# Three rewritten turns in a fused attention, experts and mixer kernel: first subtractions of two mixer pieces, one router product, three weight pieces

## The chip, the cores and the metric

One core of a Trainium2 chip runs the whole kernel as one program. The metric is the device time of one execution in microseconds (us); lower is better.

The engines are named TensorE (PE, its weight loads PEld), VectorE (DVE), ScalarE (ACT), GpSimd (POOL) and SyncE (SP, which here only issues transfers). Each runs its own instructions in order. "L1039" is line 1039 of the kernel.

## The reference

Three layers follow one another, on 2 sequences of 768 tokens with 512 channels.

```python
# attention: 8 heads of 64, 8 global keys and the last 96 keys, a slope per head
scores = q @ k.T / sqrt(64) - slope * dist          # kept keys only
x = softmax(scores) @ v
# experts: 8 experts, one for each token, by a scan over the sequence
fresh = argmax(x @ w_gate);  gate = sigmoid(x @ w_local)
e[s] = fresh[s] if s == 0 or gate[s] < 0.5 else e[s - 1]
x = p[e] * (relu(x @ w1[e]) @ w2[e])                # 512 -> 1024 -> 512
# mixer
u = x + real(fft(fft(x, axis=sequence), axis=channels))
un = (u - mean) / sqrt(var + 1e-6)
out = u + relu(un @ w_ch1) @ w_ch2                  # 512 -> 2048 -> 512
```

## The kernel before

**Split weights.** Each weight matrix is held as two parts, `hi` (a cast, on ScalarE) and `lo` (raw minus `hi`, one subtraction, L1039), and products are summed over hi*hi, hi*lo and lo*hi. `Ring.take` yields after every cast and every subtraction of one piece, so its caller decides in which place of the order each of them stands; its last step, once the raw buffer is free, issues the load of the piece four further on, from SP. Its `eng` says which engine subtracts.

**Attention** goes over 24 units (6 tiles of 128 tokens, 2 sequences, 2 groups of 4 heads), numbered n = 0 to 23. In the loop over n a unit passes through `scores` (TensorE, L133), `rowmin` (VectorE, L142), four exponentials (`expo`, ScalarE, L151), transposes `transp` in two halves (TensorE, L161), `out`, which copies each half out of PSUM to `p` (ScalarE, L167), `values` (TensorE, L175, into the upper half of the PSUM tile `sm`), `keep` (VectorE, L180), `upright` (L185) and `norm`. The units overlap: iteration n issues, in this order, `out(n-2)` second half, `keep(n-3)`, `scores(n)`, `rowmin(n)`, turn 0, first half of `transp(n-1)`, `expo(n)`, `out(n-1)` first half, turn 1, second half of `transp(n-1)`, `upright(n-3)`, `norm(n-3)`, turn 2, `values(n-2)`, turn 3. A turn is a call of `step(k)` with k = 4(n - 24) + turn. In it every background generator goes one yield further.

Two kinds of background work matter here. `Route.run(i)` is the router of tile i: it waits with `to(s)` for turn s and issues some small instructions there. For the fifth tile (i = 4, `soon`) its start is in iteration 22. The product of the gates with a unit matrix (L537, L538) goes into the lower half of `sm`; ScalarE copies it to `rows` (L541) and takes a small `exp` (L542); then come the scans `ex` (L552) and `cu` (L561) on VectorE and later the scatter of the tile's tokens to their experts' lists (L593, GpSimd). The other kind is `take` of expert 0's first three weight pieces, in quarters of 512 columns: cast on ScalarE (L1037), subtraction on GpSimd. `TAKES` gives the k at which each piece begins; a cast and a subtraction alternate from turn to turn. Their raw loads are issued in iterations 8, 12 and 16.

**The experts** follow (130 to 324 us), then the **mixer**. Its opening is an order written out by hand, `PLAN[1]`, a list of tokens; each token moves one generator by one step and names the engines of that step behind a colon (V VectorE, G GpSimd, A ScalarE):

- `f0` to `f5` fold a tile of the input (`sl0l` is the fold's `lo`, L1466)
- `q0`, `q1` are products over the sequence, `c` over the channels, `g` splits their results (`sl1l`, L1466)
- `w` is filler for TensorE
- `s` takes statistics, `k` is one instruction of the scales (the first is `v`, L1624), `n` normalises a tile to a row (L1648; `n1:A` on ScalarE, L1645), `t` turns it (transposes L1655 on TensorE, cast `un0h` and subtraction `un0l`, L1465 and L1466)
- `m0`, `m1` are the steps of the mixer's first two weight pieces: cast, subtraction, cast, subtraction (halves of 1024 columns), load. Piece 0 lies in `wide`, piece 1 in `sl5h` and `sl5l`
- `h` is the first half of the first hidden product (L1689).

The main loop then runs 48 steps, each with a hidden product (L1689, 12 matmuls of 512 columns), `hh` and `hl` (L1693 on ScalarE, L1694 on VectorE) and, after the next step's hidden product, the second product (L1703 with hh and hi, L1704 with hh and lo, L1705 with hl). Step 0 reads the first half of piece 0, step 1 the second half, steps 2 and 3 piece 1.

Of the kernel before, what the change touches and what calls it, by code (L numbers as in the profile page):

```python
# [60 lines left out]
def fast_attention(tc, st, io, route):  # L61
# [4 lines left out]
    with ExitStack() as ctx:  # L66
# [204 lines left out]
        def step(k):  # L271

            for at, g in TAKES:
                if k == at:
# [175 lines left out]
class Route:  # L450
# [31 lines left out]
    def run(self, i, xs, parts=None):  # L482
        nc, st, sb = self.tc.nc, self.st, self.sb
        V, A, G, T = nc.vector, nc.scalar, nc.gpsimd, nc.tensor
# [10 lines left out]
        last, first, soon = i == NT - 1, i == NT - 4, i == NT - 2  # L495
        X = V if last or soon else G
        to = lambda s, n=1: self.at(None if last else s, n)
# [31 lines left out]
        for b in range(B):  # L529
# [3 lines left out]
        X.tensor_tensor(pe, l8, m8[:, :, :1].to_broadcast([P, B, E]), op=ALU.subtract)  # L533
        V.scalar_tensor_tensor(gf, z.to_broadcast([P, B, E]), GATE, fr.to_broadcast([P, B, E]),
                               op0=ALU.is_lt, op1=ALU.mult)
        yield from to(1 if soon else 0, 2)
        T.matmul(rp[:, 0:P], gn.rearrange("p b e -> p (b e)"), self.identb, start=True, stop=True)  # L537
        T.matmul(rp[:, P:2 * P], gf.rearrange("p b e -> p (b e)"), self.identb, start=True, stop=True)  # L538
        rows = sb.tile([16, 2 * P], F32, name="rows")
        if not last:  # L540
            A.copy(rows, rp)  # L541
        A.activation(pe, pe, AF.Exp)  # L542
        yield from to(2 if soon else 1)
        V.tensor_reduce(out=su, in_=pe, op=ALU.add, axis=AX.X)
        if last:
            yield
# [2 lines left out]
        if last:  # L549
# [1 line left out]
        ex = sb.tile([16, P], F32, name="ex")  # L551
        V.tensor_tensor_scan(ex, rows[:, :P], (rp if last else rows)[:, P:], 0.0 if i == 0 else st.pe[:, P - 1:],  # L552
                             op0=ALU.mult, op1=ALU.add)
        yield from to(3 if soon else 2)
        V.reciprocal(su, su)
        oh = sb.tile([16, P], F16, name="oh")
        X.tensor_scalar(oh, ex, st.eid, None, op0=ALU.is_equal)
# [32 lines left out]
        for b in range(B):  # L590
            r = (i * B + b) * P
            nc.sync.dma_start(st.xs[r:r + P], xs[b])
            w = G.indirect_dma_start(  # L593
                out=st.list, out_offset=bass.IndirectOffsetOnAxis(ap=pos[:, b:b + 1], axis=0),
                in_=st.dest[:, b * NT + i], in_offset=None, bounds_check=E * LIST + P - 1, oob_is_err=False)
# [59 lines left out]
EARLY_READ = 7  # L655
EARLY_GATHER = 6
LATE = 4
TAKES = ((-43, 0), (-27, 1), (-19, 2))
SPLIT = 6
WARM = 6, 6, 3  # L660
LOAD = 6
# [4 lines left out]


PLAN = ("f0:VVVV f0:VV f0:V f1:VVVV f0:VV f1:VV", """
f2:VVVV f1:V f1:VV q0 m0:V q0 w w w q0 q0 f2:VV f2:V f2:VV q0 f3:VVVV f3:VV q0 g g g g g f4:VVVV m0:G w c c f4:VV c:VVVV c f3:V c
c:VVVV f3:VV c c s0 f5:VVVV f4:V f5:VV s1 s0 c c s3 s1 f4:VV s2 f5:V s3 s2 k k k q1 k q1 k m0 k k k k w q1  # L670
q1 k k f5:VV q1 k m1 n1:A n0:V n2:V n3:V m0:G t0 t1 g q1 m0 m1:G t2 t3 g g g m1 m1:G g m1 h
""")

DECODE, HALVE, ROOM, END = 4650, 1160, 4850, -1
# [1209 lines left out]
```

## Time and profile before

| | us |
|---|---|
| median of 3 runs | 644.39 (644.01 to 644.95) |
| profiled execution, its own time | 645.25 |
| its span, first to last instruction | 643.5 |
| attention and routing | 0 to 130 |
| experts | 130 to 324 |
| mixer's opening | 324 to 364 |
| mixer's main loop | 364 to 640 |

The profiled execution took 1.75 us more than its span. The mean granted TensorE clock over it was 0.997 of full speed. The stages are read from the timeline of TensorE.

### The profile page before, as it was taken

How to read it: one execution, taken by the hardware profiler on the slowest of the kernel's cores; microseconds unless marked ns; L12 is line 12 of the kernel's file. 1: busy time of each engine (PE TensorE's matmuls, PEld its weight loads, DVE VectorE, ACT ScalarE, POOL GpSimd, SP SyncE). 2: the span in 40 equal slices, each digit the busy share in tenths (PEclk: the TensorE clock that was granted, in tenths of full speed). 3: DMA queues.
4: the chain of work that ended last, by engine and by line, in shares of the span. 5: the costliest groups of instructions: out<-in, count | busy, mean ns of one | idle time of the engine just before them, and what ended most of it. 6: DMA issues, size and time to landing. Idle time of an engine off the chain costs nothing.

```text
span 643.5 us, 9998 instructions
## 1 busy us (share of the span) xinstructions
PE 618.0 (96%) x3634; PEld 506.6 (79%) x3635; DVE 390.0 (61%) x900; ACT 276.0 (43%) x550; POOL 111.0 (17%) x150
## 2 busy tenths in 40 slices
PE   8999988799999999999999799999999999999997
PEld 4777865498899898887867687888888888888885
DVE  5777786369875987671399877998531220272112
ACT  5788983166565565552434433541221221041110
POOL 2135562412333044210121300000000000000000
PEclk9999999999999999999999899999999999999999
DMA  8356584359887878863260143551100010100001
GB/s 304 154 200 135 135 191 158 76 181 325 317 324 258 300 248 348 347 213 115 96 261 7 66 138 125 197 196 67 65 1 1 1 67 0 66 0 1 0 1 65
DMA packets 25187, 92.45 MB, mean 144 GB/s; under 512 B 7644, under 2 KB 8796, under 8 KB 17184
## 3 DMA queue, kind: packets, MB, share of 16 engines
q1 hardware_dynamic: 19664, 79.50, 36.3%
q0 software_dynamic: 4736, 10.56, 4.5%
q10 hardware_dynamic: 720, 1.55, 0.7%
q8 instruction: 35, 0.57, 0.4%
q14 instruction: 32, 0.26, 0.2%
HBM read 81.00 MB, written 14.84 MB: 149 GB/s over the span
## 4 chain that ended last, share of the span: by engine, by line
PE 47%; issue 4%; DVE 2%; POOL 1%; ACT 0%; DVEq 0%; POOLq 0%; ACTq 0%
PE h L1689 21%; PE acc L1704 7%; PE acc L1703 7%; PE acc L1705 7%; PE y L1192 1%; PE f L1655 1%; PE more L1242 1%; PE more L1192 1%; PE h L1242 1%; PE f L1552 0%; PE f L1574 0%; POOL sl5l L1039 0%; POOL wide L1039 0%; DVE u L1714 0%; DVE fs L1477 0%
## 5 line engine op out<-in xcount | busy, mean ns | idle before, releaser
L1694 DVE SCALAR_TENSOR_TENSOR hl<-h,hh 128x512 fp32r<-128x512 f32 x48 | 33.1, 689 | 118.0 <-ACT hh L1693 117.8
L1693 ACT ACTIVATE hh<-h 128x512 fp32r<-128x512 f32 x48 | 28.7, 599 | 160.7 <-PE h L1689 160.6
L1039 DVE TENSOR_TENSOR wide<-raws,wide 128x1024 fp32r<-128x1024 f32 (+1 forms) x36 | 42.6, 1200 | 24.3 <-ACT wide L1037 23.8
L151 ACT ACTIVATE t<-t,nm 128x256 f32<-128x256 f32 (+1 forms) x96 | 45.8, 479 | 10.4 <-DVE nm L142 10.1
L1037 ACT CAST wide<-raws 128x1024 fp32r<-128x1024 f32 (+2 forms) x42 | 40.7, 990 | 6.3 <-PE acc L1705 3.4
L1689 PE MATMUL h<-un0h,wide 128*128 128x512 f32 (+1 forms) x136 | 42.5, 378 | 0.0
L1704 PE MATMUL acc<-wide,hh 128*128 128x512 f32 x96 | 37.8, 393 | 0.0
L1703 PE MATMUL acc<-wide,hh 128*128 128x512 f32 x96 | 37.6, 392 | 0.0
L1705 PE MATMUL acc<-wide,hl 128*128 128x512 f32 x96 | 37.5, 390 | 0.0
L142 DVE CUSTOM_DVE_ANT_0 t<-sp,bias 128x256 f32<-128x256 f32 (+1 forms) x96 | 33.0, 398 | 6.7 <-PE sp L133 3.5
L1122 POOL DMA_INDIRECT xg<-xs,ent x23 | 27.7, 1206 | 14.0 <-issue 6.4
L1212 PE MATMUL h<-xh,wide 128*128 128x256 f32 x192 | 28.5, 284 | 1.0 <-DVE hl L1216 0.8
L1215 ACT ACTIVATE hh<-h 128x512 fp32r<-128x512 f32 x28 | 16.7, 597 | 28.7 <-PE h L1212 21.6
L1689 PEld LDWEIGHTS h<-un0h,wide 128*128 128x128 f32 x136 | 25.0, 188 | 4.7
L161 PE MATMUL tp<-consts,t 128*128 128x128 f32 x176 | 26.4, 283 | 1.9 <-ACT p L167 1.5
L1212 PEld LDWEIGHTS h<-xh,wide 128*128 128x128 f32 x192 | 25.5, 191 | 2.0 <-DVE hl L1216 1.2
L161 PEld LDWEIGHTS tp<-consts,t 128*128 128x128 f32 x176 | 19.1, 140 | 9.9 <-ACT p L167 5.8
L175 PE MATMUL sm<-p,vs 128*64 128x128 f32 x352 | 24.5, 279 | 1.7 <-ACT rows L541 1.7
L1689 PE MATMUL h<-un0l,wide 128*128 128x512 f32 (+1 forms) x68 | 25.7, 378 | 0.0
L1216 DVE SCALAR_TENSOR_TENSOR hl<-h,hh 128x512 fp32r<-128x512 f32 x28 | 19.2, 686 | 9.2 <-issue 4.6
L167 ACT COPY p<-tp 128x512 f32<-128x512 f32 (+1 forms) x48 | 24.1, 536 | 1.2 <-PE tp L161 1.2
L175 PEld LDWEIGHTS sm<-p,vs 128*64 128x64 f32 x352 | 18.7, 136 | 5.5 <-issue 3.3
(461 smaller groups left out, 1662.4 us busy)
## 6 DMA issues: line engine op xcount, KB each, us to landing
raws<-we SPq DMA_DIRECT2D x31, 1024.0 KB
raws<-wm SPq DMA_DIRECT2D x18, 1024.0 KB
raws<-wmf SPq DMA_DIRECT2D x7, 1024.0 KB
wmf<-dec POOLq DMA_DIRECT2D x8, 512.0 KB
xs<-xrow SPq DMA_DIRECT2D x12, 260.0 KB
vs<-v SPq DMA_DIRECT2D x6, 512.0 KB
raws<-kq SPq DMA_DIRECT2D x3, 1024.0 KB
u<-x SPq DMA_DIRECT2D x6, 512.0 KB
```

The lines of the kernel that those rows point to most:

```text
L142: V.tensor_tensor_reduce(out=u.t[:, x, :u.W], in0=u.sp[:, j, k, :u.W], in1=bias[:, 4 * u.g + x, u.b0:u.b0 + u.W], scale=-0.125, scalar=3.0 ...
L151: A.activation(u.t[:, x, :u.W], u.t[:, x, :u.W], AF.Exp, bias=u.nm[:, x:x + 1], scale=-1.0, accum_out=u.den[:, x])
L161: T.transpose(u.tp[k][:, j, c], u.t[:, 2 * k + j, c * P:(c + 1) * P], st.ident)
L175: T.matmul(turned[j * D:j * D + D, k], vs[:, ti % KS, u.h + 2 * k + j], u.p[:, 2 * k + j, c], start=c == 0, stop=c == len(tiles) - 1)
L1037: (first or nc.scalar.copy)(hi[:, cs], raw[:, cs])
L1039: (eng() if callable(eng) else eng or nc.vector).tensor_tensor(lo[:, cs], raw[:, cs], hi[:, cs].bitcast(F32), op=ALU.subtract)
L1212: T.matmul(ps[:, u], w[:, f], x[:, k], start=n == 0, stop=n == 11)
L1689: nc.tensor.matmul(ps[:, c], a[:, k], x[:, k, c], start=n == 0, stop=n == 11)
L1694: nc.vector.scalar_tensor_tensor(hl, ps, 0.0, hh.bitcast(F32), op0=ALU.max, op1=ALU.subtract)
L1703: T.matmul(acc[c], hh[:, cs], h2, start=first, stop=False)
L1704: T.matmul(acc[c], hh[:, cs], l2, start=False, stop=False)
L1705: T.matmul(acc[c], hl[:, cs], h2, start=False, stop=last)
```

## The change

Three edits, all of them to the order of work.

1. In `PLAN[1]` three of the four subtractions of the mixer's pieces 0 and 1 are given to VectorE: piece 0's first, now ahead of fold 3; piece 0's second and piece 1's first, now behind the last turned rows (`t3`). Piece 1's second subtraction stays on GpSimd in its place. Piece 0's load follows its second subtraction as before.
2. In `Route.run`, for the fifth tile, the router products, the copy `rows` and the small `exp` are in turn 0 instead of 1, the sum and the scan `ex` in turn 1 instead of 2, the reciprocal and `oh` in turn 2 instead of 3.
3. In `TAKES` the three pieces of expert 0 begin at k = -53, -37 and -21 instead of -43, -27 and -19: iteration 10 turn 3, iteration 14 turn 3 and iteration 18 turn 3, instead of iteration 13 turn 1, 17 turn 1 and 19 turn 1.

```diff
-        yield from to(1 if soon else 0, 2)
+        yield from to(0, 2)
...
-        yield from to(2 if soon else 1)
+        yield from to(1)
...
-        yield from to(3 if soon else 2)
+        yield from to(2)
...
-TAKES = ((-43, 0), (-27, 1), (-19, 2))
+TAKES = ((-53, 0), (-37, 1), (-21, 2))
...
-f2:VVVV f1:V f1:VV q0 m0:V q0 w w w q0 q0 f2:VV f2:V f2:VV q0 f3:VVVV f3:VV q0 g g g g g f4:VVVV m0:G w c c f4:VV c:VVVV c f3:V c
+f2:VVVV f1:V f1:VV q0 m0:V q0 w w w q0 q0 f2:VV f2:V f2:VV q0 m0:V f3:VVVV f3:VV q0 g g g g g f4:VVVV w c c f4:VV c:VVVV c f3:V c
...
-q1 k k f5:VV q1 k m1 n1:A n0:V n2:V n3:V m0:G t0 t1 g q1 m0 m1:G t2 t3 g g g m1 m1:G g m1 h
+q1 k k f5:VV q1 k m1 n1:A n0:V n2:V n3:V t0 t1 g q1 t2 t3 m0:V g m1:V m0 g g m1 m1:G g m1 h
```

## Rows read from the trace of the kernel before

**Rows 1.** Page, part 1: busy us (share of the span) and instructions.

```profile
PE 618.0 (96%) x3634; PEld 506.6 (79%) x3635; DVE 390.0 (61%) x900; ACT 276.0 (43%) x550; POOL 111.0 (17%) x150
```

**Rows 2.** TensorE's timeline, 355 to 371: start, us, instruction, count, idle before.

```profile
355.75 0.33 PE L1515 MATMUL h<-wide,sl0l 128*1 128x386 f32 x1
359.94 1.09 PE L1655 MATMUL f<-consts,row 128*128 128x128 f32 x4 [3.85 <-issue]
...
370.54 0.39 PE L1705 MATMUL acc<-wide,hl 128*128 128x512 f32 x1
```

**Rows 3.** Windows 358 to 364: length, busy of each engine, PEclk, DMA, GB/s.

```profile
358.00:360.00 2.00, 0.06 (x1) 0.09 (x2) 1.84 (x9) 0.59 (x1) 0.00 (x0) 0.88 0.09 37
360.00:362.00 2.00, 2.00 (x10) 2.00 (x10) 1.07 (x3) 0.90 (x3) 0.00 (x0) 0.50 0.00 0
362.00:364.00 2.00, 2.00 (x13) 1.97 (x13) 1.53 (x3) 0.94 (x3) 0.00 (x0) 0.76 0.00 0
```

**Rows 4.** GpSimd's timeline, 330 to 368.

```profile
330.27 2.46 POOL L1039 TENSOR_TENSOR wide<-raws,wide 128x1024 fp32r<-128x1024 f32 x1 [2.45 <-ACT wide L1037]
351.81 2.43 POOL L1039 TENSOR_TENSOR wide<-raws,wide 128x1024 fp32r<-128x1024 f32 x1 [19.08 <-ACT wide L1037]
354.21 2.56 POOL L1039 TENSOR_TENSOR sl5l<-raws,sl5h 128x1024 fp32r<-128x1024 f32 x1
367.15 2.42 POOL L1039 TENSOR_TENSOR sl5l<-raws,sl5h 128x1024 fp32r<-128x1024 f32 x1 [10.38 <-ACT sl5h L1037]
```

**Rows 5.** VectorE's timeline, 330 to 370.

```profile
330.07 0.42 DVE L1466 TENSOR_TENSOR sl0l<-fpe,sl0h 128x257 fp32r<-128x257 f32 x1
330.41 2.60 DVE L1466 TENSOR_TENSOR sl0l<-fmo,sl0h 128x256 fp32r<-128x256 f32 x1
...
352.51 2.02 DVE L1466 TENSOR_TENSOR sl0l<-fpe,sl0h 128x257 fp32r<-128x257 f32 x1
...
354.72 2.08 DVE L1624 TENSOR_SCALAR v<-mv 128x4 f32<-128x4 f32 x1
...
364.57 1.29 DVE L1466 TENSOR_TENSOR un0l<-f,un0h 128x512 fp32r<-128x512 f32 x2 [0.88 <-ACT un0h L1465]
...
368.16 0.69 DVE L1694 SCALAR_TENSOR_TENSOR hl<-h,hh 128x512 fp32r<-128x512 f32 x1
369.10 1.55 DVE L1039 TENSOR_TENSOR sl0l<-raws,sl0h 128x1024 fp32r<-128x1024 f32 x1 [0.25 <-ACT sl0h L1037]
```

**Rows 6.** ScalarE's timeline at 366: the cast of piece 1's second half.

```profile
366.02 1.05 ACT L1037 CAST sl5h<-raws 128x1024 fp32r<-128x1024 f32 x1
```

**Rows 7.** TensorE's timeline in attention: scores of units 9, 13, 22; values of 21.

```profile
35.69 1.13 PE L133 MATMUL sp<-raws 64*128 64x256 f32 x8
...
50.63 1.13 PE L133 MATMUL sp<-raws 64*128 64x256 f32 x8
...
89.28 1.14 PE L133 MATMUL sp<-kq 64*128 64x256 f32 x8
...
97.74 1.09 PE L175 MATMUL sm<-p,vs 128*64 128x128 f32 x16 [1.70 <-ACT rows L541]
```

**Rows 8.** ScalarE's timeline in attention: two casts together; last `p` of unit 22.

```profile
54.73 1.14 ACT L1037 CAST sl0h<-raws 128x512 fp32r<-128x512 f32 x2
...
97.71 0.56 ACT L167 COPY p<-tp 128x512 f32<-128x512 f32 x1
```

**Rows 9.** TensorE's waits, 40 to 125: us in total, times, longest.

```profile
PE tp L161 <- ACT p L167: 1.5, 3, 0.9
```

**Rows 10.** GpSimd's timeline at 86: two quarters of expert 0's third piece.

```profile
86.32 2.50 POOL L1039 TENSOR_TENSOR wide<-raws,wide 128x512 fp32r<-128x512 f32 x2
```

**Rows 11.** VectorE's timeline, 53 to 88: two `cu` scans.

```profile
53.19 0.47 DVE L561 TENSOR_TENSOR_SCAN cu<-consts,cu,oh 16x128 f32<-16x128 f32 x1
...
87.45 1.64 DVE L561 TENSOR_TENSOR_SCAN cu<-consts,cu,oh 16x128 f32<-16x128 f32 x1
```

**Rows 12.** Window 77 to 78: as in rows 3.

```profile
77.00:78.00 1.00, 1.00 (x10) 0.79 (x9) 1.00 (x5) 0.86 (x4) 0.84 (x2) 1.00 0.00 0
```

More of the change, by code (lines that the diff above doesn't have):

```diff
@@ L668 @@
 PLAN = ("f0:VVVV f0:VV f0:V f1:VVVV f0:VV f1:VV", """
-f2:VVVV f1:V f1:VV q0 m0:V q0 w w w q0 q0 f2:VV f2:V f2:VV q0 f3:VVVV f3:VV q0 g g g g g f4:VVVV m0:G w c c f4:VV c:VVVV c f3:V c
+f2:VVVV f1:V f1:VV q0 m0:V q0 w w w q0 q0 f2:VV f2:V f2:VV q0 m0:V f3:VVVV f3:VV q0 g g g g g f4:VVVV w c c f4:VV c:VVVV c f3:V c
 c:VVVV f3:VV c c s0 f5:VVVV f4:V f5:VV s1 s0 c c s3 s1 f4:VV s2 f5:V s3 s2 k k k q1 k q1 k m0 k k k k w q1
-q1 k k f5:VV q1 k m1 n1:A n0:V n2:V n3:V m0:G t0 t1 g q1 m0 m1:G t2 t3 g g g m1 m1:G g m1 h
+q1 k k f5:VV q1 k m1 n1:A n0:V n2:V n3:V t0 t1 g q1 t2 t3 m0:V g m1:V m0 g g m1 m1:V g m1 h
 """)
```

## The prediction

> **What bounds the kernel now.** I read the page's share of the engines first: TensorE is busy nearly the whole span [rows 1], so a change pays where TensorE stands still or runs slowly, or moves what sets its start. Then TensorE's timeline where the mixer begins. It ends the second sequence's even products at 356.08 (355.75 + 0.33) and stands idle for 3.85 us until the first turned rows [rows 2]. The stretches show what follows: the granted clock is 0.88, 0.50 and 0.76 in the three 2 us windows from 358, so the rows were turned at 1.2 GHz [rows 3].
>
> The idle time is attributed to "issue", so no semaphore explains it. GpSimd's and VectorE's timelines do, read side by side [rows 4, 5]. GpSimd runs two mixer subtractions back to back, 351.81 to 354.24 and 354.21 to 356.77. VectorE's `sl0l` subtraction, dispatched at 352.51, ends at 354.53; the 128x4 `v` at the head of the scales, dispatched at 354.72, ends at 356.80. Each ends just after a GpSimd subtraction, and took 2.02 and 2.08 us. The same `sl0l` form takes 0.42 when GpSimd is free, and 2.60 when it meets the subtraction of 330.27 [rows 4, 5]. So GpSimd's subtraction holds VectorE up, and the scales, the normalised rows and the turned rows come after that.
>
> The rule behind it is in the Trainium skill, "SBUF — State Buffer", section "SBUF: two separate sides": the port pair that the two engines share is an exclusive lock, which the instruction that starts first keeps for its whole length, against VectorE instructions with two SBUF inputs or in a two-port mode. By that rule, the trace agrees: `hl` at 368.16, one input of which is in PSUM, keeps its 0.69 beside a GpSimd subtraction, while the `sl0l` of 369.10, with two SBUF inputs, stretches to 1.55 [rows 5]. By it the sum has both its largest gain and its largest loss (3.85 and 2.1, below); were the two engines free to run side by side, it would have neither.
>
> **Mixer, what is removed.** Three of the four subtractions leave GpSimd. Before the scales VectorE is freed of 1.60 (2.02 - 0.42) and 2.05 us (354.72 to 356.77). Further up it is freed of 2.18 (2.60 - 0.42) and takes on piece 0's first subtraction itself: 1.14 us, from the 369.10 row, which ends 1.08 after GpSimd's end, plus an estimate of 0.06 for its start. That is 1.0 us to the good. VectorE comes to the rows 3.65 to 4.65 us sooner; the idle was 3.85. I take it as closed: **+3.85**. With it goes the slow clock. The three windows lose 2 x (0.12 + 0.50 + 0.24) = 1.72 us of full clock, 0.24 of it while TensorE was idle anyway: **+1.45**. Together 5.3.
>
> **Mixer, what is added.** Behind the last turned rows VectorE now has two subtractions ahead of `hl`. I count from T, the end of the last turned rows' rest (364.57 + 1.29 = 365.86) [rows 5], to which the next hidden products are tied before and after. `hl` is due when TensorE reaches the first L1705, at T + 4.68 (370.54) [rows 2]; before, it ended at T + 2.99. Piece 0's second subtraction runs from T to T + 1.1; one `sl1l` rest, about 0.46, follows; VectorE is at piece 1's first subtraction at about T + 1.55. But piece 1's second half stays on GpSimd, and it waits only for ScalarE's cast, whose place is unchanged: cast at 366.02, GpSimd at 367.15, that is T + 1.29 [rows 4, 6]. GpSimd is ahead by some 0.25 us and holds the port to T + 3.71. Then 1.1 for the subtraction, 1.4 for three rests, 0.6 to 0.7 for `hl`: T + 6.8. TensorE waits: **-2.1**. The cover that the added work loses is the slack of `hl`, 1.7 us; without GpSimd's lead it would just do (T + 4.75). Behind the late `hl` stand piece 2's first rest and a channel step on VectorE; the second `hl` moves with TensorE, so I count nothing more. Mixer: 5.3 - 2.1 = **+3.2**. Both ends: 5.3 if VectorE comes first; 1.7 if the new idle takes the clock down too (another 1.5).
>
> The plan moves one transfer: the load behind piece 0, issued by SP once its second half is subtracted, goes from 354 to about 361. SP has nothing else to issue there, and the fifth piece, half of which it brings, is decoded only from the fourth step of the main loop on. Price nothing, behind three steps of products; were it late by x, TensorE would wait x.
>
> **Router of the fifth tile.** TensorE's longest wait in attention is 1.70 us, before the products with the values at 97.74, for ScalarE's copy `rows` [rows 7]. That copy stands behind the last unit's four exponentials and a `p` copy. A turn sooner, the router products stand right behind the last scores, and `rows` and the small `exp` ahead of those exponentials, in ScalarE's gap; the values no longer wait. But the next transposes need the last exponentials and both `p` copies. ScalarE's total is the same, and it waits some 0.4 more for the products (an estimate, for they wait on `keep`, a copy of about that length): the last copy still ends near 98.27 (97.71 + 0.56) [rows 8], the one before it 0.5 sooner. The transposes, which stand behind the values (97.74 + 1.09), can begin at about 97.9. So **+0.9**; no more than 1.7, and at worst -0.4, the shift of the exponentials. `oh` comes sooner, but `cu` keeps its turn; VectorE gets the same instructions.
>
> **Expert 0's pieces.** Nothing is added: twelve casts on ScalarE (1.14 for two) [rows 8] and twelve subtractions on GpSimd. Each piece starts 10, 10 and 2 turns sooner. Casts fall on turns 1 and 3 of a unit. Starting at turn 1, a piece put two casts between the two `p` copies of each of two units; starting at turn 3 it puts one, two, one. TensorE's waits on `p` were 1.5 us in three [rows 9], all behind pairs that now split up. The last piece also leaves the unit where its GpSimd subtractions (86.32, 2.50) hold a scan to 1.64 us; an ordinary scan is 0.47 [rows 10, 11], so 1.1 comes back on the way to the next scores. Against it, two pairs fall into units that had none: -0.6 by the mean of the old waits, 0.5, with a little for singles beside a router copy. **+2.0**. Bounds: nine units from 50.63 to 89.28 took 4.29 us each, four from 35.69 to 50.63 only 3.74 [rows 7], so at most 9 x 0.55 = 5.0; and four casts in the early units, if nothing hides them, cost 4 x 0.57 = 2.3.
>
> GpSimd's list scatters of units 14 and 18 now have no subtraction ahead of them, which I count at nothing: they are not the last. The end of attention sets the last tile's route, its gathers and the start of the experts, and TensorE then works on with hardly a pause [rows 1], so the 2.9 is passed on.
>
> **Sum.** 3.2 + 0.9 + 2.0 = 6.1. The profiled execution took 645.25 (span 643.5 and 1.75 around it): 639.15. It lies 0.86 above the median of the runs, 644.39, so the forecast is **638.3**.
>
> **Rivals.** *VectorE gets the port first.* The lead of 0.25 us rests on estimates of 0.46 and 1.1; a slightly later cast turns it. Then piece 1's subtraction runs at once, GpSimd waits, and `hl` is late by less than 0.1: 644.39 - 5.3 - 2.9 = 636.2.
>
> *The turns bring nothing in attention.* ScalarE has the same casts, and a unit with a router copy has no more room than before: only the mixer's 3.2 remains, 641.2.
>
> *No change to speak of.* The new idle takes the clock down (mixer 1.7) and the early units lose what the late ones gain, or a little more: 642.7 to 644.4, most of it within 0.2%. For it speaks that a 3.85 us idle did take the clock down [rows 2, 3]; against it, that this one is 2.1.
>
> *Slower.* The new turns are all uncovered: twelve casts of 0.57 are 6.8 us on TensorE's path, the old ones having been mostly free. It decides from 4.1 / 0.57, some seven casts uncovered; all twelve give 644.39 + 6.8 - 4.1 = 647.1. Against it: TensorE waited only 1.5 for the old casts [rows 9]. Weights that are not there yet would add to it; but in 77 to 78, just behind the last piece's new first turn, nothing is moving any more [rows 12], so at worst one cast waits a microsecond or two.
>
> **How the numbers follow.** Forecast 0.50, VectorE first 0.18, nothing in attention 0.17, no change 0.07, slower 0.08. About 0.2%, 1.3 us, is what a measurement of this kernel can tell from no change. Faster is the first three: 0.85; same 0.07; slower 0.08. The range leaves out the last two and the far tails: from 634.8 (VectorE first, and 1.4 more from the turns) to 642.6 (nothing from attention, and 1.4 less from the mixer). The likeliest case's own range is 637 to 640.
>
> **What would show it.** Right: no idle of TensorE ahead of L1655 and granted clock 1.00 from 356 to 364; `v` of 0.2; a VectorE `sl5l` of some 3 us beside GpSimd's, and TensorE waiting some 2 us at the first L1705 for `hl`; no wait of the values on `rows`; shorter waits on `p`; the experts starting some 3 us sooner. Wrong: a 1.2 us `sl5l` and no wait at L1705 (VectorE first); clock 0.50 behind that wait; waits on `p` in units 12 to 16 as long as the old ones; or the rows still late, because what held `v` was not the port.

## The result

| | median, us | runs |
|---|---|---|
| before | 644.95 | 5 (644.01 to 646.64) |
| changed | 639.41 | 5 (638.25 to 640.50) |

The ratio is 0.9910, 95% interval 0.9886 to 0.9933: faster by 5.5 us. Forecast were 638.3 us and a range of 634.8 to 642.6. The profiled execution took 639.83 us, its span is 638.1.

**A correction comes first.** The text ahead of the prediction has one letter wrong. The changed plan ends in `m1:V g m1 h`: piece 1's second subtraction goes to VectorE too. I read, and quoted, `m1:G`, as before the change. The prediction's -2.1, a collision on the last half that "stays on GpSimd", was therefore worked out for another kernel. That kernel was run as well (last_half_gpsimd, below), and it changes what the near hit is worth.

### The profile page after: what moved, and what is told of

It is laid out like the page before. It is cut to its first block, busy times and chain, and to the rows that moved or that the text cites. A ratio compares the mean times of both kernels' runs of the same rounds, so it can differ in the third digit from the quotient of the medians.

```text
span 638.1 us, 9989 instructions
## 1 busy us (share of the span) xinstructions
PE 617.1 (97%) x3634; PEld 505.3 (79%) x3635; DVE 391.1 (61%) x904; ACT 275.8 (43%) x550; POOL 101.4 (16%) x146
## 4 chain that ended last, share of the span: by engine, by line
PE 51%; DVE 2%; ACT 0%; issue 0%; DVEq 0%; ACTq 0%
PE h L1689 20%; PE acc L1704 7%; PE acc L1703 7%; PE acc L1705 7%; PE y L1192 1%; PE acc L1524 1%; PE acc L1510 1%; PE more L1242 1%; PE more L1192 1%; PE h L1242 1%; PE f L1655 1%; PE f L1552 1%; PE h L50 1%; PE f L1574 0%; DVE u L1714 0%; PE acc L1513 0%
## 5 line engine op out<-in xcount | busy, mean ns | idle before, releaser
L1039 DVE TENSOR_TENSOR wide<-raws,wide 128x1024 fp32r<-128x1024 f32 (+1 forms) x38 | 45.0, 1201 | 23.9 <-ACT wide L1037 23.4
L1705 PE MATMUL acc<-wide,hl 128*128 128x512 f32 x96 | 37.5, 390 | 0.0
L1212 PE MATMUL h<-xh,wide 128*128 128x256 f32 x192 | 28.4, 284 | 0.4 <-DVE hl L1216 0.2
L1212 PEld LDWEIGHTS h<-xh,wide 128*128 128x128 f32 x192 | 25.5, 192 | 1.2 <-ACT sl5h L1037 0.5
L1085 DVE SCALAR_TENSOR_TENSOR dec<-raws,dec 128x1024 int32<-128x1024 int32 x18 | 22.0, 1225 | 0.6
```

Of the source, the lines that this page charges most:

```text
L1039: (eng() if callable(eng) else eng or nc.vector).tensor_tensor(lo[:, cs], raw[:, cs], hi[:, cs].bitcast(F32), op=ALU.subtract)
L1212: T.matmul(ps[:, u], w[:, f], x[:, k], start=n == 0, stop=n == 11)
L1705: T.matmul(acc[c], hl[:, cs], h2, start=False, stop=last)
```

## The profile after

The page's first part: busy us, share of the span and instructions of each engine.

```profile
PE 617.1 (97%) x3634; PEld 505.3 (79%) x3635; DVE 391.1 (61%) x904; ACT 275.8 (43%) x550; POOL 101.4 (16%) x146
```

Against [rows 1] four instructions have left GpSimd and come to VectorE. TensorE's timeline where the mixer begins (start, us, instruction, count, idle before):

```profile
353.55 0.33 PE L1515 MATMUL h<-wide,sl0l 128*1 128x386 f32 x1
353.95 0.63 PE L1655 MATMUL f<-consts,row 128*128 128x128 f32 x4
354.41 0.60 PE L1655 MATMUL f<-consts,fs 128*128 128x128 f32 x4
...
355.98 1.26 PE L1655 MATMUL f<-consts,row 128*128 128x128 f32 x8
357.33 0.36 PE L1689 MATMUL h<-un0h,wide 128*128 128x256 f32 x1
...
361.82 0.50 PE L1689 MATMUL h<-un0h,wide 128*128 128x512 f32 x1 [1.39 <-DVE sl1l L1466]
...
365.14 0.39 PE L1705 MATMUL acc<-wide,hl 128*128 128x512 f32 x1
```

The idle of 3.85 [rows 2] is gone: the even products end at 353.88 (353.55 + 0.33), the turned rows start at 353.95. In its place there is a wait of 1.39 ahead of the second hidden product (step 1). VectorE's timeline says why:

```profile
350.03 0.41 DVE L1466 TENSOR_TENSOR sl0l<-fpe,sl0h 128x257 fp32r<-128x257 f32 x1
...
350.63 0.17 DVE L1624 TENSOR_SCALAR v<-mv 128x4 f32<-128x4 f32 x1
...
358.50 1.22 DVE L1039 TENSOR_TENSOR wide<-raws,wide 128x1024 fp32r<-128x1024 f32 x1
359.63 0.55 DVE L1466 TENSOR_TENSOR sl1l<-acc,sl1h 128x386 fp32r<-128x386 f32 x1
360.10 1.22 DVE L1039 TENSOR_TENSOR sl5l<-raws,sl5h 128x1024 fp32r<-128x1024 f32 x1
361.23 0.54 DVE L1466 TENSOR_TENSOR sl1l<-h,sl1h 1x386 fp32r<-1x386 f32 x1
...
362.16 1.20 DVE L1039 TENSOR_TENSOR sl5l<-raws,sl5h 128x1024 fp32r<-128x1024 f32 x1
...
363.76 0.67 DVE L1694 SCALAR_TENSOR_TENSOR hl<-h,hh 128x512 fp32r<-128x512 f32 x1
```

`sl0l` and `v` take 0.41 and 0.17, against 2.02 and 2.08 [rows 5]. Behind the turned rows stands the new work. The small split `sl1l<-h` (361.23 to 361.77) reads the PSUM tile that the last even product over the sequence left, and it queues behind two subtractions of 1.22 and another small split. The pool of tiles `h` has two buffers; step 0's product has one, and step 1's, which starts at 361.82, takes the one that the split frees. The granted clock stays at 1.00 through the wait (windows: length, busy of PE, PEld, DVE, ACT, POOL, PEclk, DMA, GB/s), where before it was at 0.50 to 0.88 [rows 3]:

```profile
358.00:360.00 2.00, 2.00 (x19) 2.00 (x18) 2.00 (x3) 2.00 (x5) 0.00 (x0) 1.00 0.03 8
360.00:362.00 2.00, 0.61 (x5) 0.41 (x4) 2.00 (x4) 1.81 (x3) 0.00 (x0) 1.00 0.62 139
362.00:364.00 2.00, 2.00 (x9) 1.62 (x10) 2.00 (x4) 0.00 (x1) 0.00 (x0) 1.00 0.91 385
```

In attention TensorE's timeline shows other waits than before. First two lines of before:

```profile
64.19 0.22 PE L537 MATMUL sm<-identb,gn 128*16 128x128 bf16 x1 [0.54 <-DVE o L180]
...
102.69 0.60 PE L868 MATMUL tp<-consts,x 128*128 128x128 f32 x4
```

The same stretch of the changed kernel:

```profile
65.09 0.22 PE L537 MATMUL sm<-identb,gn 128*16 128x128 bf16 x1 [1.27 <-DVE o L180]
...
81.84 0.22 PE L537 MATMUL sm<-identb,gn 128*16 128x128 bf16 x1 [1.28 <-DVE o L180]
...
92.15 1.13 PE L133 MATMUL sp<-kq 64*128 64x256 f32 x8
...
96.96 1.13 PE L161 MATMUL tp<-consts,t 128*128 128x128 f32 x8 [0.45 <-ACT p L167]
...
101.86 0.63 PE L868 MATMUL tp<-consts,x 128*128 128x128 f32 x4 [0.45 <-DMA x<-xs,ent]
```

The wait of the values on `rows` [rows 7] is gone, and `p` is waited for 0.7 in all, against 1.5 [rows 9]. But the router products of units 16 and 20 wait 1.27 and 1.28, where they waited 0.54 and 0.57. And the transposes of the experts' first rows (L868) wait 0.45 for a gather (the indirect DMA, issued by GpSimd, that fetches these rows); before, they started at 102.69 without a wait. GpSimd in the changed kernel beside the wait at 65.09, then VectorE in before (the first line) and in the changed kernel (the two others):

```profile
61.27 0.97 POOL L593 DMA_INDIRECT list<-dest,pos  x1 [0.30 <-issue]
62.28 0.28 POOL L528 TENSOR_SCALAR gn<-lg 128x16 bf16<-128x16 f32 x1
62.49 0.21 POOL L105 COPY raws<-gk 128x32 f32<-128x32 f32 x1
62.67 1.27 POOL L1039 TENSOR_TENSOR sl1l<-raws,sl1h 128x512 fp32r<-128x512 f32 x1
```

```profile
61.52 0.18 DVE L534 SCALAR_TENSOR_TENSOR gf<-lg,fr 128x16 bf16<-128x16 f32 x1
```

```profile
61.95 2.04 DVE L534 SCALAR_TENSOR_TENSOR gf<-lg,fr 128x16 bf16<-128x16 f32 x1
...
64.62 0.42 DVE L180 COPY o<-sm 128x256 f32<-128x256 f32 x1
```

`gf`, a 128x16 instruction of the router, has two SBUF inputs. It took 0.18 before; here it ends at 63.99, 0.05 behind a weight piece's subtraction (62.67 + 1.27). The copy `o` of `keep` is late behind it, and the router product needs `o` out of the shared PSUM tile.

**Where the time came from.** TensorE's starts at four marks, for every run: the stretch of attention from the scores of unit 6 to those of unit 23; the first product of the experts (L1212); from there to their last (L1192); from there to the first L1705, the mixer's opening.

| kernel | units 6 to 23 | first L1212 | experts | opening |
|---|---|---|---|---|
| before | 68.39 | 130.76 | 193.28 | 46.50 |
| changed | 67.52 | 130.04 | 192.34 | 42.76 |
| changed_again | 67.54 | 129.83 | 192.41 | 42.80 |
| mixer_alone | 68.36 | 131.10 | 192.26 | 42.78 |
| router_alone | 68.36 | 136.12 | 192.63 | 46.67 |
| pieces_alone | 67.53 | 131.50 | 192.81 | 46.50 |
| last_half_gpsimd | 66.79 | 128.42 | 192.77 | 47.63 |
| twice | 66.83 | 130.18 | 192.23 | 47.82 |
| pieces_between | 65.80 | 129.37 | 192.27 | 42.84 |
| split_later | 66.83 | 129.05 | 192.32 | 42.05 |
| both | 66.26 | 129.99 | 192.20 | 42.12 |
| both_without_router | 66.21 | 130.63 | 192.67 | 42.11 |
| loads_later | 66.42 | 134.70 | 192.55 | 42.14 |
| loads_later_without_router | 66.28 | 134.63 | 192.14 | 42.16 |

The spans differ by 5.4, up to the first L1705 by 5.40: 0.72 by the end of attention, 0.94 in the experts, 3.74 in the opening. The 0.94 is not the change's: mixer_alone, which leaves everything ahead of the mixer as it was, has 192.26, and the profiled execution of before is the longest of the fourteen. So in this pair the edits account for about 4.5, and 3.7 of it is the mixer's. Attention's 0.72 is the figure of one pair only. Five of these kernels have the changed attention letter for letter (changed, changed_again, last_half_gpsimd, twice, split_later); they start the experts at 128.42 to 130.18, 129.50 in the mean. The two with the old attention (before, mixer_alone) start them at 130.76 and 131.10. So attention gives 1.4 in the mean, and equal programs differ by up to 1.8 there. The opening is steadier: kernels with the same order agree within 0.2.

## The experiments

All runs were made beside runs of the kernel before on the same chip. Their medians lie 0.3 to 1.6 above the first ones, so the ratios are what is to be compared, and marks of the trace where less than a microsecond matters. Each kernel's marks come from one execution.

### Each edit by itself

mixer_alone is the kernel before with the changed `PLAN[1]`; router_alone has only the three `to(...)` of the router; pieces_alone only

```diff
-TAKES = ((-43, 0), (-27, 1), (-19, 2))
+TAKES = ((-53, 0), (-37, 1), (-21, 2))
```

> Only the edit of the mixer's opening: all four subtractions of its pieces 0 and 1 on VectorE, in the new places; attention as before. The prediction's port theory: the 3.85 us idle ahead of the turned rows and the slow clock behind it are gone without any help from attention, and with piece 1's second half on VectorE too nothing of GpSimd stands in the way, so what remains against it is VectorE's own work: the wait of 1.4 that the changed kernel shows ahead of step 1's hidden product. That gives 3.7 to 3.9 less than before, 641.1 +- 0.6, ratio 0.994. Rival (the rows were late for another reason, or the opening gained only because attention ended sooner): the idle is still there, 644 to 645.

> Only the fifth tile's router products a turn sooner. The prediction: the wait of 1.7 of the values on the copy of the router rows goes, the last transposes come 0.9 sooner, and the experts' first hidden product moves by as much: 644.0 +- 0.5, ratio 0.9986. Rival: the wait turns into another at the end of attention (on the last exponentials, or on the gather of the experts' first rows, which the changed kernel waits for 0.45), and the experts start less than 0.3 sooner: no difference.

> Only expert 0's three pieces in the new turns. The prediction: TensorE's waits on p shrink by 0.9 and blocked scans by 1.1, the last scores start 2.0 sooner, 642.9. Rival, from the changed kernel's trace: the pieces' subtractions now stand in GpSimd's queue right at the turns in which the routers of the third and fourth tile need VectorE; a 0.18 us instruction (gf) takes 2.04 there, the copy out of PSUM behind it is late, and TensorE waits 1.27 and 1.28 instead of 0.54 and 0.57 for the router product. Then 1.4 of the gain is given back: the last scores start 0.6 to 0.9 sooner, and the time is 643.9 to 644.4.

Measured: mixer_alone 0.9928 of before (0.9904 to 0.9952), 641.75 against 646.25; router_alone 0.9997 (0.9979 to 1.0016); pieces_alone 0.9975 (0.9955 to 0.9995). TensorE in mixer_alone:

```profile
354.93 0.63 PE L1655 MATMUL f<-consts,row 128*128 128x128 f32 x4
...
362.81 0.50 PE L1689 MATMUL h<-un0h,wide 128*128 128x512 f32 x1 [1.37 <-DVE sl1l L1466]
```

No idle ahead of the turned rows, the same new wait, and an opening of 42.78: the mixer's gain of 3.7 is whole without attention's help.

TensorE in router_alone:

```profile
97.67 1.13 PE L161 MATMUL tp<-consts,t 128*128 128x128 f32 x8 [0.45 <-issue]
...
104.83 0.68 PE L868 MATMUL tp<-consts,x 128*128 128x128 f32 x4 [2.48 <-DMA x<-xs,ent]
```

The last transposes come 1.1 sooner than before (98.77; 0.14 of it is that all its units stand that much earlier), as predicted. But what stands behind attention waits 2.48 for the gather: the rival's wait, and larger than in any other execution. The profiled execution is the slowest of the twelve (650.70 against a median of 646.20), so this size is not typical; that the edit alone gains nothing rests on the ratio. In pieces_alone the units run 0.86 faster, not 2.0, and the two router waits are there with 1.26 and 1.28: the rival again. The first of them:

```profile
65.11 0.22 PE L537 MATMUL sm<-identb,gn 128*16 128x128 bf16 x1 [1.26 <-DVE o L180]
```

### The port

In twice, two of the moved subtractions are also done in their old places, on GpSimd; nothing reads what they write, since VectorE writes the same values later.

```diff
-n3:V t0 t1 g q1 t2 t3 m0:V g m1:V m0
+n3:V x0 t0 t1 g q1 x1 t2 t3 m0:V g m1:V m0
...
+        def extra(m):
+            m = int(m)
+            hi, lo = ring.get("m", m)
+            raw = st.raw[ring.at["m", m] % PIECES]
+            cs = slice(1024, 2048) if m == 0 else slice(0, 1024)
+            nc.gpsimd.tensor_tensor(lo[:, cs], raw[:, cs], hi[:, cs].bitcast(F32), op=ALU.subtract)
+        self.does["x"] = extra
```

> The changed kernel with two subtractions done twice: piece 0's second and piece 1's first also on GpSimd, in their old places ahead of the turned rows, where nothing reads what they write before VectorE writes it again. No engine gets a wait of its own from them ahead of the scales. Port theory: they run from about 349.3 to 354.2, VectorE's v, dispatched at 350.6, ends behind the second of them at 354.2, the idle ahead of the turned rows is back with 3.4 to 3.9, and the clock falls behind it: 4 to 5 slower than the changed kernel. Rival (it was an order of dependences, or the place of the casts and of the load, not GpSimd's running): no idle, same time as the changed kernel within 0.5.

Measured: 1.0020 of before (1.0001 to 1.0039), against 0.9918 for changed_again beside it. GpSimd, VectorE and TensorE:

```profile
349.42 2.43 POOL L1752 TENSOR_TENSOR wide<-raws,wide 128x1024 fp32r<-128x1024 f32 x1 [23.22 <-ACT wide L1037]
351.82 2.57 POOL L1752 TENSOR_TENSOR sl5l<-raws,sl5h 128x1024 fp32r<-128x1024 f32 x1
```

```profile
350.11 2.02 DVE L1466 TENSOR_TENSOR sl0l<-fpe,sl0h 128x257 fp32r<-128x257 f32 x1
...
352.33 2.08 DVE L1624 TENSOR_SCALAR v<-mv 128x4 f32<-128x4 f32 x1
```

```profile
357.55 0.94 PE L1655 MATMUL f<-consts,row 128*128 128x128 f32 x4 [3.61 <-issue]
```

The 2.02 and the 2.08 are back to the hundredth, and the idle is back with 3.61 of 3.85, though nothing ahead of the turned rows depends on the two extra subtractions. So it is their running on GpSimd that holds VectorE, and not an order of dependences. No trace shows that what they share is a port. That is the rule of the Trainium skill, "SBUF — State Buffer", section "SBUF: two separate sides" (an exclusive lock, held for a whole instruction). The trace agrees with it: both VectorE instructions end 0.28 and 0.02 behind a GpSimd subtraction.

### The kernel that the prediction described

```diff
-m0:V g m1:V m0 g g m1 m1:V g m1 h
+m0:V g m1:V m0 g g m1 m1:G g m1 h
```

> The changed kernel with one letter different: the second subtraction of piece 1 on GpSimd instead of VectorE. It is the order of work for which the prediction worked out its term of -2.1. Port theory: GpSimd starts it at the end of its cast (359.9 in the changed kernel's time), with VectorE's first subtraction of this piece not yet begun (360.1) or just under way; in the first case VectorE stands still until 362.4 and the product of step 1 starts at 364.4 instead of 361.8, 2.6 later than in the changed kernel: 642.0. In the second case GpSimd waits until 361.3 and holds the port to 363.8 against the small splits behind it: the same place to within 0.5. Rival (the engines run side by side): VectorE has 1.1 less to do, the wait of 1.4 stays or shrinks, 639.4 or less.

Measured: 0.9975 of before (0.9955 to 0.9995). GpSimd, VectorE, TensorE, and the windows behind:

```profile
358.89 2.35 POOL L1039 TENSOR_TENSOR sl5l<-raws,sl5h 128x1024 fp32r<-128x1024 f32 x1 [33.92 <-ACT sl5h L1037]
```

```profile
358.99 3.33 DVE L1039 TENSOR_TENSOR sl5l<-raws,sl5h 128x1024 fp32r<-128x1024 f32 x1
362.25 0.54 DVE L1466 TENSOR_TENSOR sl1l<-h,sl1h 1x386 fp32r<-1x386 f32 x1
```

```profile
362.84 0.79 PE L1689 MATMUL h<-un0h,wide 128*128 128x512 f32 x1 [3.52 <-DVE sl1l L1466]
```

```profile
360.00:362.00 2.00, 0.00 (x0) 0.00 (x0) 2.00 (x1) 0.89 (x1) 1.24 (x1) 0.94 0.80 315
362.00:364.00 2.00, 1.16 (x3) 0.96 (x4) 2.00 (x5) 0.00 (x0) 0.00 (x0) 0.50 0.78 217
...
366.00:368.00 2.00, 2.00 (x6) 1.61 (x5) 1.97 (x7) 0.00 (x0) 0.00 (x0) 0.50 0.21 86
```

The collision comes as predicted: GpSimd is first, by 0.10 us (predicted 0.25), and VectorE's subtraction takes 3.33. The price is another: the wait is 3.52, at step 1's product and not at the first L1705, and TensorE then runs at 0.50, its lower level of 1.2 GHz, until past 368. The opening takes 47.63: 4.87 longer than in the changed kernel, and 1.13 longer than before.

### The new wait

split_later moves one small split ahead of piece 1's first subtraction.

```diff
-t2 t3 m0:V g m1:V m0 g g m1 m1:V g m1 h
+t2 t3 m0:V g g m1:V m0 g m1 m1:V g m1 h
```

> The changed kernel with one step of the order moved: VectorE does the small split that frees the PSUM tile of step 1's hidden product ahead of piece 1's first subtraction, not behind it. If the wait of 1.39 ahead of that product is for this tile, as the trace names it, the product starts 1.2 sooner, and TensorE then reaches the first product with hl at 363.95, where hl, behind an unchanged sum of VectorE work, ends at 364.43: a new wait of 0.5, so 0.7 faster in all. Rival (the product really waits for piece 0's second half or for hl's chain): the wait stays 1.4 and the time is the same.

Measured: 0.9897 of before (0.9875 to 0.9918); changed_again, beside it,

> The changed kernel itself once more, to stand beside the three variants of it: ratio to before 0.991 as at first. If the 0.18 us instruction gf of the third and fourth tile's router is caught by the subtraction behind it (2.04, and TensorE waits 1.27 for the router product) or not is a matter of some hundredths of a microsecond, it should again be caught in at least one of the two tiles.

0.9918 (0.9891 to 0.9945). TensorE in split_later:

```profile
359.62 0.50 PE L1689 MATMUL h<-un0h,wide 128*128 128x512 f32 x1 [0.26 <-DVE sl1l L1466]
...
363.42 0.50 PE L1705 MATMUL acc<-wide,hl 128*128 128x512 f32 x1 [0.32 <-DVE hl L1694]
```

So the wait was for that PSUM tile. It falls to 0.26, and `hl` becomes late by 0.32 (0.5 expected). The opening is 0.7 shorter: 42.05 to 42.16 in the five kernels that have this order, 42.76 to 42.84 in the four that have the changed one. The intervals of the ratios overlap; the marks don't. It is the best ratio measured.

### The pieces, the gather and the router

pieces_between puts expert 0's pieces where no subtraction stands behind a router's list scatter; both adds split_later's step to it.

```diff
-TAKES = ((-53, 0), (-37, 1), (-21, 2))
+TAKES = ((-45, 0), (-29, 1), (-13, 2))
```

> The changed kernel with expert 0's pieces begun at other turns (k = -45, -29 and -13), so that no subtraction stands in GpSimd's queue between a router's list scatter and its gf. If the subtraction is what holds gf, gf takes 0.18 in both tiles, TensorE's wait for the router product falls from 1.27 and 1.28 to 0.3 to 0.6, and the last scores start 0.8 to 1.6 sooner than in the changed kernel. Rival (gf is held by the scatter itself): gf still takes 2. What it costs elsewhere: casts come back between the p copies in other units (0.3 to 0.9 of waits), and the third piece stands in front of the gather of the experts' first rows, which may come 1 later; so 638.5 to 640, against 639.4.

> The changed kernel with both mended steps: the small split ahead of piece 1's first subtraction (mixer), and expert 0's pieces at k = -45, -29, -13 (attention). The mixer part is worth 0.8 as in split_later (1.40 of wait against 0.26 and 0.32). In attention the last scores start 1.7 sooner, but the gather of the experts' first rows, behind the 3 MB of weights that are moved from 90 to 101, lands at about 101.3 whatever attention does, so TensorE waits 1.5 for it and only 0.5 arrives at the experts: 1.3 faster than the changed kernel in all, ratio to before 0.989. If the gather does not bind, 2.5 faster, 0.987.

Measured: 0.9917 (0.9890 to 0.9945) and 0.9907 (0.9873 to 0.9940): not different from the changed kernel's by the ratios. VectorE, TensorE and a window (the last line) in pieces_between:

```profile
61.53 0.18 DVE L534 SCALAR_TENSOR_TENSOR gf<-lg,fr 128x16 bf16<-128x16 f32 x1
```

```profile
90.44 1.14 PE L133 MATMUL sp<-kq 64*128 64x256 f32 x8
...
101.35 0.63 PE L868 MATMUL tp<-consts,x 128*128 128x128 f32 x4 [1.50 <-DMA x<-xs,ent]
```

```profile
98.00:100.00 2.00, 1.85 (x18) 0.96 (x14) 0.62 (x3) 0.00 (x0) 0.87 (x2) 1.00 1.04 421
```

`gf` takes 0.18 in both tiles and the last scores start 1.7 sooner than in the changed kernel. Then TensorE waits 1.50 for the gather, and of the 1.7 only 0.5 is left at L868. The 1.7 is this execution's: the four later kernels with the same turns need 66.21 to 66.42 from unit 6 to unit 23, not 65.80, and their last scores start 1.2 to 1.3 sooner.

Two more kernels start from both and undo the router edit (both_without_router) or let SP issue 3 MB of weight loads from 103 on instead of 90 (loads_later), and one does both.

```diff
-LOAD = 6
+LOAD = 12
```

> The kernel both with the router edit undone. If the gather of the first rows is what ends attention, TensorE waits 1.7 for rows again and correspondingly less for the gather (1.5 falls to 0.6), and the time is the same as that of both within 0.3: the router edit is worth nothing there. If the gather does not bind, it is 0.9 slower than both.

> The kernel both with the 3 MB of weight loads issued behind the fifth tile's rows (at about 103) and not ahead of the gather of the experts' first rows. If those loads are what makes the gather late, it lands by 96 to 98, TensorE does not wait for it, and the products behind it (L868, L882) start 1.5 sooner than in both. The loads then share 103 to 112 with nothing urgent; the experts start 1 to 1.5 sooner: 0.987 of before. Rival (the gather has a latency of its own of about 9): the wait of 1.5 stays, same time as both; and if the loads in their new place hold up the last tile's rows or scatters, the experts start later than in both.

> The kernel loads_later with the router edit undone. With the gather out of the way the end of attention decides, so here the edit should show what the prediction gave it: TensorE waits 1.7 for rows, the last transposes are 0.9 later, and the experts start 0.5 to 0.9 later than in loads_later. Rival (the edit is worth nothing in either case): the same within 0.2.

Measured: 0.9913 (0.9879 to 0.9947), 0.9956 (0.9935 to 0.9977) and 0.9988 (0.9966 to 1.0010). TensorE, SP's queue and GpSimd in loads_later:

```profile
100.26 0.60 PE L868 MATMUL tp<-consts,x 128*128 128x128 f32 x4
```

```profile
124.35 2.14 SPq L1138 DMA_DIRECT2D ent<-list  x3
```

```profile
124.81 1.00 POOL L1119 MEMSET xg<- 128x520 f32 x2 [12.03 <-DMA xs<-xrow]
```

Without the loads ahead of it the gather, issued at 94.25, is not waited for at 100.26; with them in their old place it was issued at 93.60 and waited for until 101.46 (both), and the DMA engines are 0.94 to 1.04 busy from 94 to 100 (pieces_between). So the loads make the gather late. In their new place, though, they stand ahead of the last tile's rows (`xs<-xrow`, issued at 109.42, which GpSimd's next work waits for), the lists are read at 124.35 instead of 118.75 in both, and the experts start 4.7 later than in both (134.70 against 129.99): the second half of that expectation, at a price I had not put a number to. With the gather out of the way the router edit shows its size where the experts' first products begin (L882): 101.54 with it, 102.41 without, 0.87. But behind the late lists nothing of it is left: the experts start at 134.70 with it and at 134.63 without, where I had expected 0.5 to 0.9. With the loads in their old place the difference is 0.66 (102.76 and 103.42), not the 0.3 or less that I expected: without the edit the gather's wait did fall from 1.68 to 0.59, but the gather, issued 0.16 later, also landed 0.65 later, which stays unexplained.

## Why the prediction came out as it did

**VectorE held by the port, +3.85: right.** `v` at 0.17, TensorE's idle closed (3.78 of it); mixer_alone and twice show the cause. The fold stage, where the first subtraction moved, gives 0.54 on top (324.04 to 355.75 before, 322.38 to 353.55 after), which the prediction had left inside the closed idle.

**The slow clock, +1.45: right in kind, too large.** The clock is 1.00 throughout. From the first turned rows to the first hidden product it takes 3.38 instead of 4.16, a gain of 0.78. Up to the third tile's turned rows the gain is 1.34 (3.37 against 2.03); the last two tiles then take 0.56 longer (1.35 against 0.79), probably because they now come right behind VectorE's splits of the first two, whose PSUM tiles they need. That is read from the times and was not tested.

**The new wait, -2.1: this is the step that failed, twice over.** The letter was misread, so this collision does not happen. And for the kernel that I described, the price was wrong: "Behind the late `hl` stand piece 2's first rest and a channel step" overlooked the small split that frees step 1's PSUM tile, so the wait came one product sooner, was 3.52 and took the clock down. That order would have lost 1.1 in the mixer, not won 3.2. The real loss of 1.39 has the same root, VectorE's added work, in a place that I had not looked at. That it is of a like size as the 2.1 is luck, and so is much of the near hit.

So the mixer gave 3.74 (0.54 + 3.78 + 0.78 - 1.37, the last being what the first L1705 lost from there on), against 3.2.

**The fifth tile's router, +0.9: right where it stands, not at the end.** The transposes gain 0.93 (96.96 against 97.89 in pieces_alone). By L868 nothing is left (101.86 against 101.82), since the gather of the first rows ends there. No pair of runs shows the edit in the whole time (0.9997 in router_alone; 0.9907 against 0.9913 in both with and without it).

**Expert 0's turns, +2.0: 0.86 measured.** The gains that were counted came: the longest wait on `p` is 0.45 instead of 0.9. The failed step is "I count at nothing" for the list scatters that no longer have a subtraction ahead of them. They come sooner, `gf` of the router comes beside them, and the next subtraction stands right behind. Being caught costs 0.70 each time: 67.5 from unit 6 to 23 with both caught (three executions), 66.8 with one (three). Without either the turns would by that have given 2.3 (an estimate, 0.86 + 2 x 0.70; the turns of pieces_between, where neither is caught, give 2.0 to 2.6).

**"The 2.9 is passed on": wrong.** 0.72 arrived in the profiled pair, 1.4 in the mean of the five executions. For transfers I had looked at 77 to 78 [rows 12] alone; the busy stretch is 90 to 101, and the gather lies in it. In last_half_gpsimd, the one of the five that did not wait for the gather, 2.3 arrived (128.42 against 130.76).

The total of 6.1 against 5.4 in the two profiled executions is thus made of a mixer taken 0.5 too low, for the wrong reason, an attention taken 2.2 too high (1.5 by the mean of the five), and 0.94 that the execution of before had lost among the experts.

## What to carry to other kernels

An instruction on GpSimd that is off the critical path need not be free while VectorE works beside it (here 3.85 us of TensorE's time): look for short VectorE instructions that end just behind a long GpSimd one. When work is moved onto an engine, walk through every instruction behind it in that engine's queue, also the small ones that only free a PSUM tile, and ask who starts on it. A gain ahead of a transfer is worth only what the transfer's landing leaves, so look at what else is on the queues when it is issued; and quote the change letter by letter before costing it.

## What was not expected of the hardware

Whether `gf` is caught goes with hundredths of a microsecond. With the changed turns it is seen twelve times in six executions. In the nine where it started 0.67 or 0.68 us behind the second scatter's start, it took 2.02 to 2.04 and ended behind the subtraction, which is the third GpSimd instruction after the scatter; in the three where it started 0.66 behind, it took 0.17 or 0.18. So VectorE did not get in where these GpSimd instructions follow each other, not even in the one gap that the trace has (62.24 to 62.28 in the changed kernel). What in the scatter decides it, the runs don't show.

An idle of 1.39 left the granted clock at 1.00, and one of 3.52 took it to 0.50 for about 7 us (0.94 in the window from 360, 0.50 in the three from 362, 0.85 in the one from 368); so the second cost TensorE 2.1 more of wait, and 2.7 more (4.87 - 2.13 in the opening) at the lower level.
